# Attention in portions behind fixed VectorE and TensorE work, and other sums moved in a transformer block: a prediction and its test

## The chip, the cores and the metric

The kernel runs on one core of a Trainium2 chip. The metric is the device time of one execution in microseconds (us). The core has engines that work side by side, each through its own queue in order: TensorE (PE in the profile) multiplies matrices, VectorE (DVE) and ScalarE (ACT) work on elements, GpSimd (POOL) here mostly issues transfers (DMAs), SyncE (SP) here issues only transfers.

A ratio is the mean time of one kernel's fast runs over that of the kernel before in the same rounds on the same chip, so it is not quite the ratio of the medians that I quote beside it.

## The reference, cut to what matters

```python
xn = layernorm(x)                                   # 2048 tokens x 1024
q, k, v = split(xn @ wqkv)                          # 32 heads of 32
logits = einsum(q, k at 8 earlier positions, 2 apart) * 32**-0.5
attn   = softmax(logits)                            # over the 8 positions
s = einsum(attn, v at the same positions) @ wo
g = silu((silu(xn @ w1) * (xn @ w3)) @ w2)          # 1024 -> 3584 -> 1024
return x + s * g
```

The large products run on TensorE. Attention looks at only eight positions, so it has no large product: it is VectorE work.

## The kernel before

Tokens are handled in two halves of 1024, each half in two chunks of 512. The stages follow in this order: qkv, first up (w1 and w3), first down (w2), first wo; then the second half: up, wo, down. Every large product is done by Winograd's form of Strassen's scheme: seven products of half size in place of eight, with sums of the operands. VectorE makes these sums, also those of the weights, so VectorE stands between TensorE and its operands in each block:

```python
def seven(key, A, B, e11, e12, e22, e21, snap=None):      # one block: 56 matmuls
    ...
    for i in I: mm(pb[:, i], s2[i], t2, False)
    act_copy(su2[:], pb[:])
    for i in I: mm(pe[:, i], s4[i], b22, False)
    e12(pe, su2)          # VectorE: um = em + um;  in qkv: a pk sum
    for i in I: mm(pb[:, i], s3[i], t3, False)
    e22(pb, sp5)          # VectorE: h_sb = bm + pm;  in qkv: a pk sum
    def tail(): ...       # last product, into pb, three products later
```

`pe` and `pb` are PSUM tiles (PSUM is the memory that the matmuls write into). In the profile the first letter is that of the tile and the second that of the stage: `bm` and `em` are `pb` and `pe` of an up stage, `aq`, `bq` and `eq` tiles of qkv, and names with d or w in front tiles of down and wo. The tail writes into `pb`, so TensorE waits until the VectorE sum `h_sb` has read it; likewise `pe` comes free by `um`.

The queue order of an engine is made by a scheduler at build time. `issue_after` (here `behind`) holds an instruction behind another one in that order:

```python
def w_sums(fb):                      # sums of w1/w3 of block fb
    with behind(("m", fb - 1)):      # behind the um sum of the block before
        nc.vector.tensor_add(sa[:, 0], a21, a22)   # L547 in the profile
        ...                          # three more, then stores to s_dram

def w2_step(fb):                     # sums of w2, for two blocks at a time
    if fb % 2 == 0:
        ...                          # load two ring slots of w2
        return
    with behind(("t", fb)):          # behind the h_sb sum of block fb
        nc.vector.tensor_sub(o1, b12, b11)         # L618
        ...                          # three more, then the store to t_dram

def park(t, c, j0, name):            # q, k, v of chunks 1 to 3 go to HBM
    tl = k4(name, (2, CH), BF16)     # one of four small buffers
    def fin():
        m = nc.scalar.dma_start(out=dst, in_=tl[:])            # ACT's queue
        ...

def fetch_k(c):                      # k and q of a chunk come back
    nc.gpsimd.tensor_copy(out=kT[:, :, 0:HALO], in_=kT[:, :, CH:CH + HALO])
    nc.gpsimd.dma_start(out=kT[:, :, HALO:], in_=k_dram[c])
    qt[c] = att_tile((NJ, CH), BF16, f"qt{c}")
    nc.gpsimd.dma_start(out=qt[c][:], in_=q_dram[c])
```

The four small buffers that q, k and v pass through are called `pk` in the profile. A `pk` sum or copy writes one, so it has to wait until the store that last read this buffer has landed.

Attention is issued in a few large steps at a low priority (`priority(BG + ...)`), and VectorE takes them between the other sums as the scheduler decides. The weights go through a ring of nine slots: a slot is loaded again when its last reader, or the store of what was made in it, is done.

Of the kernel before, what the change touches and what calls it, by code (L numbers as in the profile page):

```python
# [17 lines left out]
def kernel(  # L18
# [126 lines left out]
    def mm(ps, lhs, rhs, first):  # L145
        n = len(lhs)
        for k in range(n):
            nc.tensor.matmul(  # L148
                ps, lhsT=lhs[k], rhs=rhs[k], start=(first and k == 0),
                stop=(k == n - 1), skip_group_check=not first,  # L150
            )
# [28 lines left out]
    def seven(key, A, B, e11, e12, e22, e21, snap=None):  # L180
# [27 lines left out]
        e22(pb, sp5)  # L208

# [119 lines left out]
    def park(t, c, j0, name):  # L329
        tl = k4(name, (2, CH), BF16)  # L330
        dst = (q_dram, k_dram, v_dram)[t][c, :, j0:j0 + 2, :]

        def fin():
            m = nc.scalar.dma_start(out=dst, in_=tl[:])
            if spill:
                d, f = spill.pop(0)
                with tc.issue_after(m.ins):
                    nc.scalar.dma_start(out=d, in_=f)

        return tl[:], fin  # L340
# [6 lines left out]
    def qkv_copy(t, c, j0):  # L347
        def f(ps, *a):
            d, fin = qkv_dst(t, c, j0)
            with hp():  # L350
                if a:
                    nc.vector.tensor_add(d, ps[:], a[0][:])
                else:
                    anchor["c", t, c, j0] = nc.scalar.copy(out=d, in_=ps[:])  # L354
                fin()
        return f
# [29 lines left out]

    def fetch_k(c):
        if c == 0:
            return
        nc.gpsimd.tensor_copy(out=kT[:, :, 0:HALO], in_=kT[:, :, CH:CH + HALO])  # L390
        nc.gpsimd.dma_start(out=kT[:, :, HALO:], in_=k_dram[c])
# [3 lines left out]
    def fetch_v(c):  # L395
        nc.gpsimd.tensor_copy(out=vT[:, :, 0:HALO], in_=vT[:, :, CH:CH + HALO])
        nc.gpsimd.dma_start(out=vT[:, :, HALO:], in_=v_dram[c])

    def scores(c):
        q = qt[c]  # L400
        E = att_tile((W, CH), BF16, f"Es{c}")
        for w in range(W):
            o = HALO - DIL * w
            p_t = att_tile((NJ, CH), BF16, f"pt{c}_{w}")
            nc.vector.tensor_mul(p_t[:], q[:], kT[:, :, o:o + CH])  # L405
            nc.vector.tensor_add(p_t[:, 0:4, :], p_t[:, 0:4, :], p_t[:, 4:8, :])  # L406
            nc.vector.tensor_add(p_t[:, 0:2, :], p_t[:, 0:2, :], p_t[:, 2:4, :])
            nc.vector.tensor_add(E[:, w, :], p_t[:, 0, :], p_t[:, 1, :])
        sc[c] = E

    def score_sums(c):
        E = sc[c]
        zp = bank2(f"zp{c}")
        for h in range(2):
            for sq in range(4):
                nc.tensor.matmul(
                    zp[sq * 32:(sq + 1) * 32, h].rearrange("p (w t) -> p w t", t=P), lhsT=ones4[:],
                    rhs=E[:, h * 4:(h + 1) * 4, sq * P:(sq + 1) * P], start=True, stop=True,
                )
        sc[c] = E[:].bitcast(FP32).rearrange("p w n -> p (w n)").rearrange("p (a w t) -> p a w t", a=2, t=P)  # L420
        nc.scalar.copy(out=sc[c][:, 0], in_=zp[:].rearrange("p h (w t) -> p (h w) t", t=P))

    def softmax(c):
        Z = sc[c]
        z, zm, zs = Z[:, 0], Z[:, 1, 0:4], Z[:, 1, 4:8]
# [4 lines left out]
        nc.scalar.activation(out=z, in_=z, func=ACTF.Exp, scale=scale)  # L430
# [8 lines left out]
    def values(c, pairs=(0, 2, 4, 6)):  # L439
        E = pr[c]  # L440

        def pvmul(dst, w):
            o = HALO - DIL * w
            nc.vector.tensor_mul(dst, E[:, w, :].unsqueeze(1).to_broadcast([P, NJ, CH]), vT[:, :, o:o + CH])  # L444

        A = oT[:, c % 2]
        for w0 in pairs:
            B = att_tile((NJ, CH), BF16, f"B{c}_{w0}")
            if w0 == 0:
                pvmul(A, 0)  # L450
                pvmul(B[:], 1)
            else:
                C = att_tile((NJ, CH), BF16, f"C{c}_{w0}")
                pvmul(B[:], w0)
                pvmul(C[:], w0 + 1)
                nc.vector.tensor_add(B[:], B[:], C[:])
            nc.vector.tensor_add(A, A, B[:])  # L457

    def att_steps():
        with priority(BG - 10000):  # L460
            scores(0)
        yield
        score_sums(0)
        fetch_k(1)
        with priority(BG):
            softmax(0)
            scores(1)
            values(0)
            fetch_v(1)
        yield  # L470
        with priority(BG + 9000):
            fetch_k(2)
        yield
        score_sums(1)
        with priority(BG + 10000):
            softmax(1)
            scores(2)
            values(1)
            fetch_k(3)
            fetch_v(2)  # L480
        yield
        score_sums(2)
        with priority(BG + 20000):
            softmax(2)
        yield
        with priority(BG + 30000), behind("wo"):
            scores(3)
            values(2, (0, 2, 4))
        yield
        score_sums(3)  # L490
        with priority(BG + 40000):
            softmax(3)
            values(2, (6,))
            fetch_v(3)
            values(3)
        yield

    att_it = att_steps()

    def att_step():  # L500
        next(att_it)
# [17 lines left out]
    def up_load(b, fb):  # L519
# [7 lines left out]
        else:  # L527
            up_sums(b, fb, w1t, w3t)
            sa, s4 = tiles[b, fb][2:]
            nc.sync.dma_start(out=sa[:], in_=s_dram[fb, :, 0:2])  # L530
            nc.sync.dma_start(out=s4[:], in_=s_dram[fb, :, 3])
# [3 lines left out]
    def up_sums(b, fb, w1t, w3t):  # L535
        sa = r4(("sa", fb), (2, KH, 2 * P), FP16)
        half.append(half.pop(0))
        s4 = slot(5, (KH, 2 * P), FP16, half[0] * SLOT // 2)
        tiles[b, fb] = w1t, w3t, sa, s4

    def w_sums(fb):
        up_sums(0, fb, *tiles[0, fb])
# [3 lines left out]
        with behind(("m", fb - 1)):  # L546
            nc.vector.tensor_add(sa[:, 0], a21, a22)  # L547
            nc.vector.tensor_sub(sa[:, 1], sa[:, 0], a11)
            nc.vector.tensor_sub(s4[:], a12, sa[:, 1])
            nc.vector.tensor_sub(s3, a11, a21)  # L550
# [11 lines left out]
    def mlp_up(b, steps={}):  # L562
        order = [*range(b * FB // 2, FB - 1), *range(b * FB // 2), FB - 1]
        for n, fb in enumerate(order):
            steps.get(n, lambda: None)()
            if n == 0:
                up_load(b, fb)
                if b == 0:
                    w_sums(fb)
                up_load(b, order[1])  # L570
# [8 lines left out]
            def e12(pe, su2):  # L579
# [5 lines left out]
                if b == 0:  # L585
                    anchor["m", fb] = m
                    if fb + 1 < FB:
                        w_sums(fb + 1)
                if n + 2 < FB:
                    up_load(b, order[n + 2])  # L590

            def e22(pb, sp5):
                with hp():
                    m = nc.vector.tensor_add(h_sb[:, f2, CH:], pb[:], sp5[:])  # L594
                if b == 0:
                    anchor["t", fb] = m
                    w2_step(fb)

            def e21(pb, f2=f2, hl=hl, n=n, fb=fb):
                release(("w3", fb))  # L600
                with hp():
                    nc.scalar.copy(out=hl["g"][:, :, 0:CH], in_=pb[:])  # L602
                    nc.vector.tensor_mul(h_sb[:, f2, :], h_sb[:, f2, :], hl["g"][:])  # L603

            seven(f"m{b}_{fb}", up_A(b, fb), B0, e11, e12, e22, e21)

    def w2_step(fb):
        if fb % 2 == 0:
            tiles["t"] = [r4("t", (2, 2, CH)) for x in range(2)]
            for x in range(2):  # L610
                nc.sync.dma_start(out=tiles["t"][x][:], in_=w2_q[:, fb:fb + 2, x])
            return
        q = tiles["t"]
        q16 = [t[:].bitcast(FP16) for t in q]
        b11, b12, b21, b22 = [q[x][:, :, y] for x in range(2) for y in range(2)]
        o1, o3, o4, o2 = [q16[x][:, :, y] for x in range(2) for y in range(2)]
        with behind(("t", fb)):
            nc.vector.tensor_sub(o1, b12, b11)  # L618
            nc.vector.tensor_sub(o3, b22, b12)
            nc.vector.tensor_sub(o2, b22, o1)  # L620
            nc.vector.tensor_sub(o4, b21, o2)
        for x in range(2):
            nc.gpsimd.dma_start(out=t_dram[:, fb - 1:fb + 1, 2 * x:2 * x + 2], in_=q16[x])
        release("t")
# [13 lines left out]
    def mlp_down(b, done=lambda *a: None, mid=lambda n: None):  # L638
        NQ = (0, 4, 8, 11, 14)

        def rhs_tiles(kind, fh=0, dh=0, t=0):
            key = kind, fh, dh, t
            ops = [key]
            for f0, f1 in zip(NQ, NQ[1:]):
                wt = r4(key, (f1 - f0, CH), FP16 if kind == "t" else BF16)
                if kind == "t":
                    nc.sync.dma_start(out=wt[:], in_=t_dram[:, f0:f1, t, :])
# [23 lines left out]
        def sums(gp):  # L671
# [3 lines left out]
            with hp():  # L675
                for g in G2:
                    nc.vector.tensor_add(s1[g], a21[g], a22[g])
                for g in G2:
                    nc.vector.tensor_sub(s3[g], a11[g], a21[g])

# [5 lines left out]
        for gp in G2:  # L686
            act_copy(pb[gp][:], pa[gp][:])
            with hp():
                nc.vector.tensor_sub(s2[gp], s1[gp], a11[gp])
        rhs = rhs_tiles("w", 1, 0)  # L690
        product(pa, lst(a12), rhs, False)
        rhs = rhs_tiles("t", t=T2)
        for gp in G2:
            with hp():
                nc.vector.tensor_sub(s4[gp], a12[gp], s2[gp])
# [5 lines left out]

        product(pb, lst(s2), rhs, False, snap2)
        mid(0)
        for gp in G2:
            with hp():
                silu(g_tile(b, 0, 0, gp), pa[gp][:])
            done(0, 0, gp)
        rhs = rhs_tiles("t", t=T3)
        product(pb, lst(s3), rhs, False)
# [3 lines left out]
        def c22(gp):  # L713
            sp5 = k4(f"dsp{b}_{gp}")
            act_copy(sp5[:], pe[gp][:])
            with hp():
                nc.vector.tensor_add(sp5[:], pb[gp][:], sp5[:])
                silu(g_tile(b, 1, 1, gp), sp5[:])
            done(1, 1, gp)

        product(pe, lst(s1), rhs, True, c22)
# [255 lines left out]
```

## Time and profile before

| | before |
|---|---|
| time, median of 3 runs | 754.03 us |
| span of the profiled run | 754.6 us |
| TensorE busy | 726.5 us, 96% |
| VectorE busy | 619.8 us, 82% |
| mean granted TensorE clock | 0.991 |

The profiled run took 756.28 us.

The head of the page of the kernel before: span, busy time of each engine with its share and number of instructions, and then the span in 40 slices, busy tenths for PE and DVE and the granted clock of TensorE in tenths.

```profile
span 754.6 us, 8791 instructions
...
PE 726.5 (96%) x3367; PEld 346.4 (46%) x3367; DVE 619.8 (82%) x602; ACT 312.9 (41%) x327; POOL 95.1 (13%) x156
...
PE   8999999889999999999899999999999999999997
...
DVE  7997996789999999999899558999984999552143
...
PEclk9999999999999999999999999999999999999999
```

TensorE is the bound, and it can only be won back where it stands still. The waits of PE of the kernel before: who waited for whom, total us, number of waits, the longest.

```profile
PE bm L148 <- DVE h_sb L594: 7.0, 9, 1.6
PE aq L148 <- ACT bq L158: 6.2, 3, 3.3
PE am L148 <- ACT bm L158: 2.3, 6, 0.5
PE da L148 <- DMA wring<-in_B_w_dram: 2.3, 1, 2.3
```

The first line is TensorE waiting for `h_sb`; VectorE had attention in front of it. The second is the end of qkv. The chain of waits of the kernel before in that stretch (start, duration, what) shows who was behind it:

```profile
135.20 4.94 DMA wring<-in_B_w_dram
...
140.23 0.06 DVE wring L547
...
143.04 1.23 DVE pk L352
...
144.35 1.01 ACT bq L158
...
145.40 1.89 PE aq L148 x8
```

VectorE's queue had the first weight sum (L547) ahead of a `pk` sum. The load of its weights took 4.9 us; then came the weight sum and an attention product of 2.3 us (L405, at 140.84 us), the `pk` sum stood behind both, and ACT and TensorE behind that. An instruction that waits at the head of an in-order queue holds up everything behind it. The Trainium skill says the same of these engines ("TensorE: Matmul & The Clock Gate", Part 1, on queue depths: VectorE is strict FIFO), and this chain agrees.

The stretches with a lower clock are three records of 3.4 us at clock 0.5, at 161, 366 and 529 us; such a stretch costs 1.7 us of TensorE work. They are called half clock below.

### The profile page before, as it was taken

The numbers are of one execution on the slowest core, as the hardware profiler recorded it, in microseconds if no ns is written. First come the engines' busy times: TensorE is split into PE (matmuls) and PEld (weight loads), VectorE is DVE, ScalarE is ACT, GpSimd is POOL, SyncE is SP. The second block draws the span as 40 slices with busy tenths as digits, with TensorE's granted clock in tenths as the row PEclk, the third lists the DMA queues.
The fourth block names the chain that finished last, engine by engine and source line by source line (L and its number), as shares of the span: only waits on it lengthen the run. The fifth ranks groups of instructions, "written<-read, shape, count | busy, mean of one in ns | idle before, by whom it ended". The sixth has DMA issues, their size and how long they took to land.

```text
span 754.6 us, 8791 instructions
## 1 busy us (share of the span) xinstructions
PE 726.5 (96%) x3367; PEld 346.4 (46%) x3367; DVE 619.8 (82%) x602; ACT 312.9 (41%) x327; POOL 95.1 (13%) x156
## 2 busy tenths in 40 slices
PE   8999999889999999999899999999999999999997
PEld 4655555444444444434344444444444444444443
DVE  7997996789999999999899558999984999552143
ACT  5744344435444555443021443443565454420121
POOL 0000001320211253411001402000022000000000
PEclk9999999999999999999999999999999999999999
DMA  8366358844778899979575978554367543624631
GB/s 324 122 153 197 125 168 294 271 146 166 230 244 258 274 320 303 308 243 330 190 229 182 354 228 282 163 162 129 121 183 235 152 132 120 209 83 140 207 115 56
DMA packets 130218, 153.68 MB, mean 204 GB/s; under 512 B 14976, under 2 KB 100480, under 8 KB 129536
## 3 DMA queue, kind: packets, MB, share of 16 engines
q1 hardware_dynamic: 112960, 102.25, 44.0%
q0 software_dynamic: 11024, 37.76, 14.8%
q10 hardware_dynamic: 6192, 13.11, 4.7%
q8 instruction: 26, 0.43, 0.2%
q14 instruction: 16, 0.13, 0.1%
HBM read 107.48 MB, written 39.32 MB: 195 GB/s over the span
## 4 chain that ended last, share of the span: by engine, by line
DVE 44%; PE 36%; issue 12%; DMA 5%; ACT 1%; POOL 0%; SPq 0%; DVEq 0%; ACTq 0%; POOLq 0%
PE bq L148 5%; DVE pt L405 5%; PE db L148 5%; PE da L148 5%; PE bm L148 4%; DVE B L444 3%; PE de L148 3%; DVE oT L457 3%; DVE um L581 3%; PE am L148 3%; DVE h_sb L594 3%; PE aq L148 3%; DVE pt L406 3%; PE eq L148 3%; PE em L148 3%
## 5 line engine op out<-in xcount | busy, mean ns | idle before, releaser
L148 PEld LDWEIGHTS <-wring 128*128 128x128 f16 (+1 forms) x1952 | 205.1, 105 | 232.1 <-issue 19.8
L148 PE MATMUL bm<-xs,wring 128*128 128x512 f16 x672 | 156.5, 380 | 7.1 <-DVE h_sb L594 7.0
L148 PEld LDWEIGHTS <-h_sb 128*128 128x128 f16 (+1 forms) x976 | 103.0, 106 | 121.7 <-issue 12.7
L148 PE MATMUL am<-xT,wring 128*128 128x512 bf16 x448 | 107.3, 382 | 2.3 <-ACT bm L158 2.3
L405 DVE TENSOR_TENSOR pt<-qt,kT 128x4096 bf16<-128x4096 bf16 x32 | 73.1, 2287 | 1.0 <-ACT kT L354 0.4
L148 PE MATMUL db<-wring,h_sb 128*128 128x512 f16 x336 | 73.3, 379 | 0.0
L583 ACT ACTIVATE g<-um 128x1024 bf16<-128x1024 f32 x28 | 29.6, 1057 | 86.4 <-DVE um L581 82.1
L437 POOL DMA_DIRECT2D Ep<-pb x64 | 37.0, 586 | 128.2 <-DVE pb L433 120.7
L148 PE MATMUL em<-xs,wring 128*128 128x512 f16 x224 | 52.9, 379 | 0.0
L148 PE MATMUL da<-wring,h_sb 128*128 128x512 bf16 x224 | 50.7, 388 | 2.3 <-DMA wring<-in_B_w_dram 2.3
L148 PE MATMUL em<-xT,wring 128*128 128x512 bf16 x224 | 52.9, 379 | 0.0
L603 DVE TENSOR_TENSOR h_sb<-h_sb,g 128x2048 bf16<-128x2048 bf16 x28 | 34.1, 1217 | 8.0 <-ACT g L602 8.0
L406 DVE TENSOR_TENSOR pt<-pt 128x2048 bf16<-128x2048 bf16 x32 | 38.9, 1219 | 0.4
L577 ACT ACTIVATE h_sb<-am 128x1024 bf16<-128x1024 f32 x28 | 28.7, 1024 | 21.5 <-PE am L148 21.5
L158 ACT COPY pm<-em 128x1024 f32<-128x1024 f32 x28 | 28.3, 1011 | 21.1 <-PE em L148 21.1
L581 DVE TENSOR_TENSOR um<-em,um 128x1024 f32<-128x1024 f32 x28 | 34.0, 1216 | 3.2 <-PE em L148 3.2
L158 ACT COPY um<-bm 128x1024 f32<-128x1024 f32 x28 | 28.4, 1014 | 19.9 <-PE bm L148 19.9
L457 DVE TENSOR_TENSOR oT<-oT,B 128x4096 bf16<-128x4096 bf16 x16 | 36.5, 2283 | 0.1
L444 DVE TENSOR_TENSOR B<-Ep,vT 128x4096 bf16<-128x4096 bf16 x16 | 36.4, 2282 | 0.0
L602 ACT CAST g<-bm 128x1024 bf16<-128x1024 f32 x28 | 28.3, 1012 | 16.1 <-PE bm L148 15.8
L594 DVE TENSOR_TENSOR h_sb<-bm,pm 128x1024 bf16<-128x1024 f32 x28 | 34.0, 1214 | 0.4 <-PE bm L148 0.4
L158 ACT COPY bm<-am 128x1024 f32<-128x1024 f32 x28 | 28.0, 1002 | 10.1 <-PE am L148 10.0
(180 smaller groups left out, 886.5 us busy)
## 6 DMA issues: line engine op xcount, KB each, us to landing
wring<-in_B_w_dram SPq DMA_DIRECT2D x68, 512.0 KB, 5.6
wring<-t_dram SPq DMA_DIRECT2D x16, 512.0 KB, 4.6
s_dram<-wring POOLq DMA_DIRECT2D x14, 512.0 KB, 3.7
s_dram<-wring POOLq DMA_DIRECT2D x28, 256.0 KB, 4.8
t_dram<-wring POOLq DMA_DIRECT2D x14, 512.0 KB, 6.9
wring<-s_dram SPq DMA_DIRECT2D x28, 256.0 KB, 3.1
wring<-s_dram SPq DMA_DIRECT2D x14, 512.0 KB, 3.9
wring<-in_A_wqkv_dram SPq DMA_DIRECT2D x6, 1024.0 KB, 7.5
```

Of the source, the lines that this page charges most:

```text
L148: nc.tensor.matmul(ps, lhsT=lhs[k], rhs=rhs[k], start=(first and k == 0), stop=(k == n - 1), skip_group_check=not first,)
L158: nc.scalar.copy(out=out_, in_=in_)
L405: nc.vector.tensor_mul(p_t[:], q[:], kT[:, :, o:o + CH])
L406: nc.vector.tensor_add(p_t[:, 0:4, :], p_t[:, 0:4, :], p_t[:, 4:8, :])
L437: nc.gpsimd.dma_start(out=pr[c][r:P:NR, :, sq * P:(sq + 1) * P], in_=pb[sq * 32:(sq + 1) * 32, :, :])
L444: nc.vector.tensor_mul(dst, E[:, w, :].unsqueeze(1).to_broadcast([P, NJ, CH]), vT[:, :, o:o + CH])
L457: nc.vector.tensor_add(A, A, B[:])
L577: nc.scalar.activation(out=h_sb[:, f2, 0:CH], in_=pa[:], func=ACTF.Silu)
L581: m = nc.vector.tensor_add(su2[:], pe[:], su2[:])
L583: nc.scalar.activation(out=hl["g"][:, :, CH:], in_=su2[:], func=ACTF.Silu)
L594: m = nc.vector.tensor_add(h_sb[:, f2, CH:], pb[:], sp5[:])
L603: nc.vector.tensor_mul(h_sb[:, f2, :], h_sb[:, f2, :], hl["g"][:])
```

## The change

Its intent: attention no longer comes in large steps, but in portions of so many us of VectorE work for each block of TensorE work, queued behind the block's fixed sums. The weight sums stand behind each block's first sum; the w2 sums are issued two blocks later; the stores of q, k, v go to SP's queue; the residual is copied into the output first and the results are added to it by the transfer; wo of the second half comes last. The core of the diff, with cuts marked by "...":

```diff
@@ seven
         e22(pb, sp5)
+        bg(pace["n"])
@@ park
-            m = nc.scalar.dma_start(out=dst, in_=tl[:])
+            m = nc.sync.dma_start(out=dst, in_=tl[:])
@@ attention
+    def bg(us):                       # issue about so many us of attention
+        ...
+        with priority(BG), behind("v"):
+            while pace["credit"] > 0:
+                t = next(att_it)
+                ...
-    def values(c, pairs=(0, 2, 4, 6)):
+    def values(c):                    # chunks 0 and 2 in two halves
+        ...
     def fetch_k(c):
-        nc.gpsimd.dma_start(out=kT[:, :, HALO:], in_=k_dram[c])
+        anchor["pool"] = nc.gpsimd.dma_start(out=kT[:, :, HALO:], in_=k_dram[c])
         qt[c] = att_tile((NJ, CH), BF16, f"qt{c}")
         nc.gpsimd.dma_start(out=qt[c][:], in_=q_dram[c])
@@ w_sums
-        with behind(("m", fb - 1)):
+        with behind("v"):
             nc.vector.tensor_add(sa[:, 0], a21, a22)
-            nc.vector.tensor_sub(sa[:, 1], sa[:, 0], a11)
-            ...
+        nc.vector.tensor_sub(sa[:, 1], sa[:, 0], a11)
+        ...
@@ mlp_up: in the tail of block fb
+                if b == 0:
+                    w2_sums(fb - 2)
+                    w2_load(fb)
@@ w2
-        with behind(("t", fb)):
-            nc.vector.tensor_sub(o1, b12, b11)
-            ...
+    def w2_sums(fb):                  # one block, half the width
+        ...
+        nc.vector.tensor_sub(o1, b12, b11)
+        ...
@@ results
-            nc.vector.tensor_add(g, g, xw[u, dh][:, gp])
-            nc.gpsimd.dma_start(out=out_rows(out_flat, 0, u, dh, gp), in_=g)
+            nc.gpsimd.dma_start(out=out_rows(out_flat, b, u, dh, gp), in_=g, accum_op=ALU.add)
@@ end of qkv k
-    xn_sums(xT1[:, 0], xT1[:, 1], xT1[:, 2], xT1[:, 3], xs1)
+    with behind("u"):
+        xn_sums(xT1[:, 0], xT1[:, 1], xT1[:, 2], xT1[:, 3], xs1)
@@ program
-    mlp_up(1, {0: att_step, 6: att_step})
-    wo_prepare(1)
-    wo(1, finish1)
-    residual()
-    mlp_down(1, gated)
+    pace["n"] = 8.3
+    mlp_up(1)
+    mlp_down(1, lambda: mid(1), (7, 10, 10, 9, 9, 3))
+    wo(1)
```

Note two things: the anchor of the w2 sums (`behind(("t", fb))`; an anchor is the instruction that another one is held behind) is taken away and has no successor, and nothing holds the load of q, whose line is unchanged.

## The prediction

> **What bounds the kernel now.** TensorE. The page's busy table has PE 96% busy (726.5 of 754.6 us), DVE 82%. In the chain of waits a product of 112 matmuls takes 24.17 us, 215.8 ns each, and both programs hold the same 3367 matmuls. So the change can only win time in which PE stands still or runs slowly. From the waits of PE and the timeline:
> - PE behind an ACT copy that waits for a late VectorE `pk` sum, at 142 and 157 us: 5.5 us. In the chain, VectorE's queue holds the MLP's first weight sum ahead of those `pk` sums, and that sum waits 4.9 us for weights.
> - PE behind the VectorE sum `h_sb` (bm<-h_sb), in both up stages: 7.0 us; behind ACT bm copies 2.3 us. VectorE is busy 20 of 20 us there (windows), with attention in front of the short sums.
> - PE in the first down product behind a weight load: 2.3 us; its ring slot waited for the w2 sums' store.
> - Three stretches of 3.4 us at half clock, at 161, 366 and 529 us, each just after such stalls (windows: granted clock 0.91): 1.7 us each. The Trainium skill, "TensorE: Matmul & The Clock Gate", Part 1, says the clock drops to half after an idle window of about 3.4 us; this trace shows drops after stalls of 2 us, and it decides.
> - Smaller ones, 2 us. Head (30 us) and tail (5.4 us after the last matmul) stay.
> Within reach: some 24 us. Floor near 730 us.
>
> **What the change does.** It issues attention in portions behind fixed sums, so that `pk`, `um`, `h_sb` are never behind more than about one 2.3 us operation. In the changed program's queue order the last `pk` sums stand before the first weight sum, and block 0's weights load earlier, between the q and v stores. w2 sums come two blocks late, so ring slots are free before down. wo of the second half goes last: same PE work.
> VectorE, with before's durations: residual sums fall away (-11 us); w2 sums at half width, 4 x 0.42 for one block instead of 4 x 0.68 for two, +4 us; values of chunks 0 and 2 in halves (1.22 instead of half of 2.28), +5 us. Net near zero.
> Balance of a block (PE: 56 x 0.2158 = 12.1 us): first up stage 3 x 1.22 + 4 x 0.68 + 4 x 0.42 + 4.5 attention = 12.5 us: slightly too much, I keep 2 to 3 us of stalls there. Second up stage 3.65 + 8.3 = 11.95: fits. Down: room for 7 to 10 us per product.
> Stores move from ACT's queue to SP's: ACT is no longer held up; weight loads can queue behind a store, estimated at no PE time.
> Tail: the last sum reads PSUM directly, in two halves; about the same 5.4 us. The earlier accumulating stores end, I estimate, shortly before it.
>
> **Result.** 754 - 7 (qkv end, with clock) - 4 (down) - 5 (second up stage, with clock) - 3 (first up stage, rest) = 735 us. Range 730 to 742. Chances: faster by over 2% 0.70, within 2% 0.28, slower 0.02.
>
> **What would show it.** PE waits at 140 to 160 us gone; da<-DMA gone; bm<-h_sb under 3 us; at most one half-clock stretch; DVE busy about 617 us, spread through the last 110 us; wo last, about 5 us before the end.
>
> **What would make it wrong.** A portion that waits (k, v or weights from DMA) at the head of VectorE's queue; SP holding weight loads behind a store; VectorE falling behind in the first up stage, each stall over 2 us costing another 1.7 us of clock; attention of chunk 1 or 3 late before wo; accumulating stores that end last.

## The result

| | before | changed |
|---|---|---|
| time, median (lowest to highest) | 754.10 us (753.07 to 754.72, 4 runs) | 759.37 us (757.82 to 760.22, 4 runs) |
| ratio, 95% interval | | 1.0069 (1.0048 to 1.009) |
| span of the profiled run | 754.6 us | 756.1 us |
| after the last matmul | 5.4 us | 7.8 us |

The changed kernel is 0.7% slower; I had put 735 us with a range up to 742. Executions over 1.5% slower than the fastest of the same kernel are left out of the means. The profiled run of the changed kernel is its fastest of four, and the profiled run of the kernel before is slower than its four, so the spans of the two profiles lie closer than the medians.

The head of the page of the changed kernel, the lines as before:

```profile
span 756.1 us, 8856 instructions
...
PE 724.1 (96%) x3367; PEld 346.7 (46%) x3367; DVE 619.6 (82%) x646; ACT 314.0 (42%) x326; POOL 110.1 (15%) x173
...
PE   8997999999998998998899999999999999999995
...
DVE  8984789589988888979799874696999799999515
...
PEclk9998999999999999999999999999999999999999
```

Busy times say nothing here: they are the same. The PE row says where to look: the right half is all nines, the left half has holes. The windows of the changed kernel (columns: PE, PEld, DVE, ACT and POOL busy us with instructions, granted clock, DMA share, GB/s) put numbers to it:

```profile
60.00:80.00 20.00, 15.59 (x62) 8.03 (x61) 11.53 (x10) 5.58 (x6) 0.00 (x0) 0.83 0.53 169
...
280.00:300.00 20.00, 16.59 (x70) 7.07 (x69) 16.92 (x23) 9.41 (x10) 2.70 (x5) 0.91 0.73 236
340.00:360.00 20.00, 16.83 (x71) 7.25 (x72) 18.50 (x21) 7.09 (x7) 6.22 (x11) 0.91 0.91 284
...
380.00:740.00 360.00, 359.94 (x1678) 162.57 (x1677) 293.06 (x235) 138.53 (x136) 42.37 (x54) 1.00 0.59 178
```

From 380 us on TensorE does not stand still for even 0.1 us in 360. The portions do there what they are meant to. What was won there and at the end of qkv was lost before 380 us, mostly to waits that the kernel before did not have. The waits of PE of the changed kernel:

```profile
PE em L148 <- DVE wring L604: 7.3, 3, 4.7
PE eq L148 <- DVE h_sb L289: 4.4, 1, 4.4
PE bm L148 <- DVE h_sb L650: 4.2, 2, 3.4
PE da L148 <- DMA wring<-in_B_w_dram: 2.6, 1, 2.6
...
PE bq L148 <- DVE pk L354: 1.4, 1, 1.4
```

and the two lines of the waits of DVE that stand behind them:

```profile
DVE wring L677 <- DMA wring<-in_B_w_dram: 17.1, 7, 4.7
...
DVE pk L354 <- DMA k_dram<-pk: 11.1, 1, 11.1
```

L677 is the first of the four w2 sums. VectorE stood 17 us at its head, waiting for w2 to be loaded. The timeline of DVE of the changed kernel shows one of these seven waits (start, duration, what, and in brackets the idle time before it):

```profile
231.28 1.22 DVE L638 TENSOR_TENSOR um<-em,um 128x1024 f32<-128x1024 f32 x1
232.41 0.68 DVE L604 TENSOR_TENSOR wring<-wring 128x1024 f16<-128x1024 bf16 x1
235.96 0.42 DVE L677 TENSOR_TENSOR wring<-wring 128x512 f16<-128x512 bf16 x1 [2.87 <-DMA wring<-in_B_w_dram]
236.30 1.22 DVE L650 TENSOR_TENSOR h_sb<-bm,pm 128x1024 bf16<-128x1024 f32 x1
```

This is the fifth L638 and the fifth L677: the w2 sum of the block stands between the block's own `um` and `h_sb`, not two blocks later. And `h_sb` (L650), for which TensorE waits, stands behind it. So does the weight sum L604 behind which TensorE waits longest: the w2 sum at 334.06 us came after a wait of 4.7 us, L604 only at 342.43 us, after work that had queued up meanwhile, and TensorE stood still from 338.5 to 343.2 us. The chain of waits of the changed kernel in the same stretch goes one step further back:

```profile
223.91 3.44 DMA s_dram<-wring
...
227.48 8.39 DMA wring<-in_B_w_dram
...
235.96 0.10 DVE wring L677
...
236.30 1.22 DVE h_sb L650
```

The w2 load waits for its ring slot, which comes free by the store of the block's weight sums. So w2 arrives late, in seven of the 14 blocks, and in this chain the wait starts in VectorE's own sums.

The second loss, at 69 us. The chain of waits of the changed kernel there:

```profile
54.29 1.24 DVE pk L354
55.52 2.63 SPq L286
...
59.42 7.44 DMA k_dram<-pk
...
67.75 1.23 DVE h_sb L289
...
69.02 1.04 PE eq L148 x2
```

L286 is a transfer on SP's queue that transposes the normalised x (a transposing load below); the k store now stands behind four of these. A later `pk` sum waits 11 us for the buffer that this store reads, and the xn sums (L289), which TensorE waits for, stand behind the `pk` sum. A stretch of 6.8 us at half clock begins at 67 us, within the stall.

The records of the granted clock of the changed kernel show half clock at 67 us (6.8 us) and at 289 and 344 us (3.4 us each): 13.6 us in all before the tail, against 10.2 us before.

### The profile page after: what moved, and what is told of

The parts are those of the page before. It is cut to its first block, busy times and chain, and to the rows that moved or that the text cites. A ratio compares the mean times of both kernels' runs of the same rounds, so it can differ in the third digit from the quotient of the medians.

```text
span 756.1 us, 8856 instructions
## 1 busy us (share of the span) xinstructions
PE 724.1 (96%) x3367; PEld 346.7 (46%) x3367; DVE 619.6 (82%) x646; ACT 314.0 (42%) x326; POOL 110.1 (15%) x173
## 4 chain that ended last, share of the span: by engine, by line
PE 74%; DVE 9%; DMA 8%; issue 5%; ACT 1%; POOL 1%; SPq 1%; DVEq 0%; POOLq 0%; ACTq 0%
PE bm L148 14%; PE em L148 10%; PE db L148 10%; PE am L148 9%; PE bq L148 6%; PE de L148 6%; PE da L148 6%; DMA wring<-in_B_w_dram 4%; PE eq L148 4%; PE aq L148 3%; PE wb L148 2%; DMA s_dram<-wring 2%; PE wa L148 2%; PE we L148 1%; DVE stats L244 1%
## 5 line engine op out<-in xcount | busy, mean ns | idle before, releaser
L469 DVE TENSOR_TENSOR BC<-Ep,vT 128x2048 bf16<-128x2048 bf16 (+1 forms) x42 | 65.1, 1573 | 0.2
L148 PE MATMUL em<-xs,wring 128*128 128x512 f16 x224 | 55.7, 394 | 7.3 <-DVE wring L604 7.3
L638 DVE TENSOR_TENSOR um<-em,um 128x1024 f32<-128x1024 f32 x28 | 34.1, 1219 | 15.1 <-PE em L148 13.0
L454 POOL DMA_DIRECT2D Ep<-pb x64 | 37.0, 588 | 56.9 <-PE bm L148 51.2
L479 DVE TENSOR_TENSOR oT<-oT,BC 128x2048 bf16<-128x2048 bf16 (+1 forms) x24 | 37.8, 1573 | 0.3
L650 DVE TENSOR_TENSOR h_sb<-bm,pm 128x1024 bf16<-128x1024 f32 x28 | 34.1, 1219 | 2.6 <-PE bm L148 2.6
L354 DVE TENSOR_TENSOR pk<-eq,uq 128x1024 bf16<-128x1024 f32 x12 | 14.7, 1222 | 25.6 <-PE eq L148 12.2
```

The costliest lines, as they stand in the source:

```text
L148: anchor["pe"] = nc.tensor.matmul(ps, lhsT=lhs[k], rhs=rhs[k], start=(first and k == 0), stop=(k == n - 1), skip_group_check=not first,)
L454: nc.gpsimd.dma_start(out=pr[c][r:P:NR, :, sq * P:(sq + 1) * P], in_=pb[sq * 32:(sq + 1) * 32, :, :])
L469: nc.vector.tensor_mul(dst, E[:, w, :].unsqueeze(1).to_broadcast([P, n, CH]), vT[:, js, o:o + CH])
L479: nc.vector.tensor_add(A, A, B if w0 else C)
L638: m = nc.vector.tensor_add(su2[:], pe[:], su2[:])
L650: m = nc.vector.tensor_add(h_sb[:, f2, CH:], pb[:], sp5[:])
```

## The experiments

In the edits below, "A" is the changed kernel and "B" the kernel before. My theory was that there are two misplacements: stores on SP behind the transposing loads, and w2 sums ahead of `h_sb`. The rivals: VectorE has too much work in the first up stage (12.5 us for 12.1 us of TensorE by my own sum in the prediction), or transfers get in each other's way. All kernels gave a correct result, except the one that is wrong on purpose.

| run | edit | median us | ratio (95%) |
|---|---|---|---|
| changed | | 759.37 | 1.0069 (1.0048 to 1.009) |
| a_store_act | A, stores on ACT's queue | 758.27 | 1.0069 (1.0039 to 1.0099) |
| a_w2_late | A, w2 sums behind the next block's h_sb | 738.34 | 0.9817 (0.9799 to 0.9835) |
| a_store1_w2 | the same, and stores of chunk 1 on ACT | 735.29 | 0.9764 (0.9748 to 0.978) |
| b_store_sp | B, stores on SP's queue | 750.46 | 0.9964 (0.9941 to 0.9987) |
| a_nou | A, xn sums without anchor | 755.01 | 1.0026 (0.9994 to 1.0059) |
| a_nou_w2 | a_w2_late and a_nou | 737.44 | 0.979 (0.9763 to 0.9816) |
| a_nou_store1_w2 | a_store1_w2 and a_nou | 740.82 | 0.9844 (0.9818 to 0.9871) |
| b_w2_free | B, w2 sums without anchor | 762.54 | 1.0127 (1.0097 to 1.0156) |
| a_qt | A, q load behind k load | 755.65 | 1.0029 (0.9997 to 1.0061) |
| a_qt_w2 | a_w2_late and a_qt | 737.07 | 0.9796 (0.9772 to 0.9821) |
| a_qt_w2_plain | the same, last stores do not add (wrong result) | 734.41 | 0.976 (0.9735 to 0.9785) |
| a_qt_w2_res | a_qt_w2, residual copy later | 740.03 | 0.9834 (0.9802 to 0.9865) |
| a_qtmid_w2 | a_w2_late, q load near 116 us | 732.75 | 0.9739 (0.9723 to 0.9755) |
| a_qtmid_nou_w2 | the same and a_nou | 732.18 | 0.9733 (0.9713 to 0.9753) |

### The w2 sums: a_w2_late and b_w2_free

```diff
@@ A, after the h_sb sum
+                if b == 0:
+                    anchor["h", fb] = m
@@ w2_sums
-        nc.vector.tensor_sub(o1, b12, b11)
+        with behind(("h", min(fb + 1, FB - 2))):
+            nc.vector.tensor_sub(o1, b12, b11)
```

> The changed kernel with each block's w2 sums held behind the next block's h_sb sum in VectorE's queue (at the latest behind that of block 12). Theory: the 17 us that VectorE waits for w2 loads fall below 3 us, em behind the weight sum (7.3 us), bm behind h_sb (4.2 us) and two half-clock stretches (3.4 us) nearly go: time 759 minus 10 to 15, 744 to 749. Rival (VectorE is overfull in the first up stage: 12.5 us of work for 12.1 us of TensorE in each block): only a third of it goes, time 754 or more, because the work itself is unchanged.

Measured: 738.34 us, 19 us by the ratios (1.0069 to 0.9817 of 754), more than I had put down. VectorE's waits for w2 loads fell from 17.1 to 2.1 us. In the waits of PE of this kernel the line of `em` behind the weight sum is gone, and of the 4.2 us behind `h_sb` 0.4 are left; the stall at 69 us stays.

```profile
PE eq L148 <- DVE h_sb L289: 4.5, 1, 4.5
...
PE da L148 <- DMA wring<-in_B_w_dram: 1.2, 1, 1.2
PE bq L148 <- DVE pk L354: 1.1, 1, 1.1
...
PE bm L148 <- DVE h_sb L650: 0.4, 1, 0.4
```

The same VectorE work in another order: the rival of the overfull VectorE falls. Two half-clock stretches went with the stalls; only the one at 69 us is left. The mirror of it takes the anchor from the kernel before:

```diff
@@ B, w2_step
-        with behind(("t", fb)):
+        with nullcontext():
```

> The kernel before with the anchor of its w2 sums taken away, so that the scheduler may place them as early as in the changed kernel; nothing else. Theory (the place of w2 sums in VectorE's queue is what costs): VectorE then waits for w2 loads 8 us or more and TensorE behind um, h_sb or weight sums in the first up stage by 5 us or more beyond the 5 us of before: time 753 plus 4 to 12. Rival (the harm is special to the changed kernel, its rings and loads): within 2 us of 753.

Measured: 762.54 us, 9.7 us slower, in the range given. VectorE waits 10.7 us for w2 loads. The timeline of DVE of this kernel has the longest one, and the waits of PE what it cost:

```profile
289.32 0.69 DVE L618 TENSOR_TENSOR wring<-wring 128x1024 f16<-128x1024 bf16 x1 [8.18 <-DMA wring<-in_B_w_dram]
...
291.83 1.22 DVE L581 TENSOR_TENSOR um<-em,um 128x1024 f32<-128x1024 f32 x1
292.97 0.68 DVE L547 TENSOR_TENSOR wring<-wring 128x1024 f16<-128x1024 bf16 x1
```

```profile
PE em L148 <- DVE wring L547: 10.0, 3, 7.8
```

The `um` sum and the weight sum L547 stand behind a w2 sum that waits 8.2 us, and TensorE waits 7.8 us for that weight sum. So the missing anchor does the same harm in a kernel that has nothing else of the change, though it costs about half as much there, 9.7 us in place of 19. That the place of the w2 sums is what costs is settled: one anchor, there and not there, in both kernels.

### The stores' queue: a_store_act, b_store_sp, a_store1_w2

```diff
@@ a_store_act: A, park          (b_store_sp is the reverse, in B)
-            m = nc.sync.dma_start(out=dst, in_=tl[:])
+            m = nc.scalar.dma_start(out=dst, in_=tl[:])
     ... and the same for the stores of x and xs
@@ a_store1_w2: A with the edit of a_w2_late, and
-            m = nc.sync.dma_start(out=dst, in_=tl[:])
+            m = (nc.scalar if t < 2 and c == 1 else nc.sync).dma_start(out=dst, in_=tl[:])
```

> The changed kernel with its q, k, v and spill stores back on ACT's queue, nothing else. Theory (two misplacements: stores queued on SP behind the four transposing loads, and w2 sums that stand in VectorE's queue ahead of sums whose turn it is): VectorE's 11.1 us wait for a k_dram store at 55 to 67 us falls below 2 us, the TensorE stall of 4.4 us at 69 us and its two half-clock windows go, time 759 minus 6 to 8, 751 to 753; the stalls of the first up stage stay. Rival (VectorE has too much attention in this stage, the queue of the stores is innocent): the stall at 69 us stays above 3 us and the time within 2 us of 759.

Measured: 758.27 us, no gain that the intervals show. The stall at 66 us shrank from 4.4 to 1.9 us, between what theory and rival had put down, but VectorE still waited 7.6 us for the k store, and another stall, of 2.1 us with half clock, came at the end of qkv.

> The kernel before with its stores on SP's queue, nothing else of the change. Theory (the queue of the stores alone makes the stall at 69 us): the same stall of 4 us or more appears near 69 us, with a half-clock window, time 754 plus 5 to 8. If stores on ACT's queue were what hurt the end of qkv, the stall of 5.5 us at 142 to 160 us falls at the same time; I expect it to stay, since VectorE's wait for weights makes it. Rival: no stall at 69 us, time within 2 us of 754 or lower.

Measured: 750.46 us, a little faster, and no stall above 0.7 us near 69 us. So my theory of the store's queue falls: it does no harm there alone. The second part of the expectation was wrong too: the stalls at 142 and 157 us did not stay, and one of 4.1 us with 6.8 us of half clock came at 165 us. In this kernel's timeline of DVE the `pk` sums (138.59 and 139.73 us) stand ahead of the weight sum (140.86 us), so the edit moved more than the stores: the order of VectorE's sums changed with it.

> Both mends: the q and k stores of chunk 1, those in the time of the transposing loads, go to ACT's queue, all other stores stay on SP's, and w2 sums behind the next block's h_sb. Theory: the gains add, 759 minus 17 to 22, 737 to 742, TensorE stalls after 30 us under 5 us in all. Rival (contention of transfers or too much VectorE work): less than 10 us gained.

Measured: 735.29 us, in the range, 0.5% better than a_w2_late. But a_store_act and b_store_sp forbid me to read that as the store's queue in general. Something else in the changed kernel had to make the store late.

### The anchor of the xn sums: a_nou, a_nou_w2, a_nou_store1_w2

```diff
@@ A
-    with behind("u"):
+    with nullcontext():
         xn_sums(xT1[:, 0], xT1[:, 1], xT1[:, 2], xT1[:, 3], xs1)
```

> The changed kernel without the one anchor that holds the sums of the second half's xn (h_sb by four sums) behind the k sums of chunk 1; stores stay on SP's queue, w2 sums as changed. In VectorE's order this moves just those four sums ahead of one pk sum. New theory (the stall at 69 us needs both: a pk sum that waits 11 us for a buffer whose store is late, and the xn sums placed behind it): the stall of 4.4 us and its two half-clock windows go, time 759 minus 6 to 8, 751 to 753, although the late store is still there and VectorE still waits for it 4 us or more. Rival (the late store alone): the stall stays above 3 us.

Measured: 755.01 us, short of the 751 to 753 put down; by the ratios 3.2 us less than the changed kernel, with intervals that overlap. The stall of 4.4 us turned into two of 2.0 and 1.2 us, without half clock: the xn sums now stand first, but they themselves wait 4.8 us for a transposing load.

> w2 sums held behind the next block's h_sb, and the xn sums' anchor taken away. Theory: the gains add to the 738.3 us of the first alone: minus 5 to 7, 731.5 to 733.5; TensorE stalls from 30 us on under 4 us in all, no half-clock window before the tail. Rival for the size: if a stall only moves to the next wait, time 735 or more.

Measured: 737.44 us: not the 731.5 to 733.5 put down. The rival for the size was right: the stall went to the next wait (2.3 us at 69 us, with its half clock).

> As the run before it, with the q and k stores of chunk 1 on ACT's queue too. Theory: with the xn sums ahead of it, the late store harms nothing, so within 1 us of that run. Rival (the store's queue counts by itself): 2 us or more faster.

Measured: 740.82 us, a miss on both sides: slower than a_nou_w2. The xn sums waited 9.5 us for the transposing loads, of which the last landed at 64.9 us, against 60.4 us in a_nou_w2. With stores on ACT's queue these loads were later in three kernels; why, I did not find out. But all three pointed to one thing: the last transposing loads are late in every descendant of the changed kernel so far. They landed at 60.5 us in the changed kernel, at 56.5 us in b_store_sp, which shares the stores' queue. (In the kernel before they landed at 60.3 us, as late. But there the k stores did not stand behind them: issued on ACT's queue, they had landed by 59.5 us.)

### The load of q: a_qt, a_qt_w2, a_qtmid_w2, a_qtmid_nou_w2

In the changed kernel POOL issues the 1 MB load of q for chunk 1 at 52 us; in the kernel before at 117 us. Nothing in the new source holds it, and q is in HBM by then. At 52 us the last two transposing loads run.

```diff
@@ a_qt: A, fetch_k
-        nc.gpsimd.dma_start(out=qt[c][:], in_=q_dram[c])
+        with behind("pool"):                  # behind the load of k
+            nc.gpsimd.dma_start(out=qt[c][:], in_=q_dram[c])
```

> The changed kernel with the load of q for chunk 1 (1 MB, issued at 52 us there, at 117 us before) held behind the load of k for the same chunk; nothing else. Third theory for the stall at 69 us: this load runs beside the last two transposing loads and makes them land after 7 us in place of 3.3, and the stores behind them on SP's queue go late with them. Expected: the last transposing load lands before 57 us in place of 60.5, TensorE's stall there below 1.5 us, no half-clock window before the first up stage, time 759 minus 5 to 8. Rivals (the store's queue; the anchor of the xn sums): the stall stays above 3 us, since both are still as changed.

Measured: 755.65 us. The last transposing load landed at 56.9 us, 3.1 us after its issue in place of 7.0, and the k stores behind it started at 55.8 us in place of 58.9. TensorE's stall there is 0.9 us and no half clock follows, although the store's queue and the anchor were as in the changed kernel. Only the start of the store moved: each k store takes 7.4 to 7.6 us in both kernels (7.7 in b_store_sp, 3.5 in the kernel before; why is not shown), and VectorE still waits 7.6 us for it, in place of 11.1. The time missed its range: by the ratios 3 us less than the changed kernel in place of 5 to 8, since stalls of 1.0 and 2.0 us came at 148 and 167 us, and the wait at 370 us (2.7 us, 2.6 in the changed kernel) was now followed by half clock.

Here is the timeline of SP in the changed kernel, and then in a_qtmid_w2 (below), where the q load is elsewhere too: the same four transposing loads hold SP 9.0 us in the one and 5.7 us in the other, and the k stores behind them start at 58.9 and 55.7 us.

```profile
49.17 8.98 SPq L286 DMA_TRANSPOSE h_sb<-wring  x4
...
58.87 0.93 SPq L335 DMA_DIRECT2D k_dram<-pk  x2
```

```profile
49.28 5.66 SPq L286 DMA_TRANSPOSE h_sb<-wring  x4
...
55.66 0.95 SPq L335 DMA_DIRECT2D k_dram<-pk  x2
```

The Trainium skill ("DMA: Bandwidth & Descriptors", "Issuing engines are not separate DMA queues") says that transfers issued by SP, ACT and POOL run on the same 16 DMA engines and interleave. This agrees: with the load from POOL's queue beside them the last two loads from SP's took 7.4 and 7.0 us (changed kernel), without it 3.2 and 3.1 (a_qt).

So the stall of 4.4 us takes both: the stores on SP's queue without the early q load left 0.7 us (b_store_sp) and 0.9 us (a_qt), the early q load with the stores on ACT's queue 1.9 us (a_store_act).

> The same, and w2 sums held behind the next block's h_sb. Theory: 738.3 minus 5 to 7 of the w2 run alone, 731 to 734, TensorE stalls after 30 us under 4 us in all, no half-clock window before the tail. If the stall at 69 us only turns into another wait: 736 or more.

Measured: 737.07 us, again the gain did not add. The stall near 69 us was down to 1.1 us, and others came up at 148 us (1.3 us) and 167 us (2.1 us, with half clock). Behind the k load the q load now ran from 134.9 to 145.1 us, beside the v stores and the first MLP weights; a v store, issued at 136.4 us, landed 8.9 us later, where the same store took 6.3 us in a_w2_late and, as it turned out, 6.4 us in a_qtmid_w2. The `pk` buffers came free late, and a `pk` sum waited 9.1 us for one. The same harm at another place, though with more traffic around it. So the next two kernels put the load where little else runs:

```diff
@@ a_qtmid_w2: A with the edit of a_w2_late, and
@@ park
             m = nc.sync.dma_start(out=dst, in_=tl[:])
+            anchor["st", t, c, j0] = m
@@ fetch_k
-        nc.gpsimd.dma_start(out=qt[c][:], in_=q_dram[c])
+        if c == 1:
+            with behind(("st", 2, 1, 2)):     # behind a v store
+                nc.sync.dma_start(out=qt[c][:], in_=q_dram[c])
+        else:
+            nc.gpsimd.dma_start(out=qt[c][:], in_=q_dram[c])
```

> w2 sums behind the next block's h_sb, and the load of q for chunk 1 on SP's queue between the v stores, near 105 us: away from the transposing loads (52 us), and away from the k load and the first MLP weights (135 us, where a_qt_w2 put it). Theory (a 1 MB load beside the stores that pk buffers wait for is what stalls TensorE, wherever it stands): TensorE stalls of 60 to 175 us fall below 3 us with no half-clock window before the tail; ratio to before 0.972 to 0.976, against 0.982 of w2 alone and 0.980 of a_qt_w2. Rival (the stall only moves on again): ratio 0.979 or more.

Measured: 732.75 us, ratio 0.9739, as the theory had it (the load was issued at 116 us, as in the kernel before). TensorE's stalls from 60 to 175 us are 1.0 us at 66 us and 1.0 us at 165 us, and there is no half-clock stretch between 6 and 726 us. It beats the kernel before by 2.6%. The edit changes two things about the load, its time and its queue (SP's in place of POOL's); no run parts them.

> The same without the anchor that puts the xn sums behind a pk sum. Theory: with the transposing loads early, the xn sums start at 57 us and the stall of about 1 us at 66 us goes too; ratio 0.970 to 0.975. Rival (the anchor costs nothing by then): within 0.002 of the run before it.

Measured: 732.18 us, ratio 0.9733. The stall at 66 us went, another of 0.2 us came at 68 us, and the one at the end of qkv grew to 1.6 us. Within 0.002: the anchor has no part of its own that these runs can show.

### The tail and the first down product: a_qt_w2_plain, a_qt_w2_res

```diff
@@ a_qt_w2_plain: the stores of the second half's first six results
-            nc.gpsimd.dma_start(..., in_=g, accum_op=ALU.add)
+            nc.gpsimd.dma_start(..., in_=g)
@@ a_qt_w2_res
-            if c == 0:
-                residual(0)
             yield from values(c + 1)
+            if c == 0:
+                residual(0)
```

In this expectation "the run before it" is a_qt_w2.

> Wrong result on purpose (second half without the residual): as the run before it, but the stores of the second half's first six results do not add to what lies in memory. Theory (the adding stores slow the last four stores): the last four land within 1.8 us of issue as before, in place of 2.3 to 3.4, and the time falls by 1 to 1.5 us against the run before it. Rival (the tail is VectorE's and the number of stores): change under 0.4 us.

Measured: 734.41 us, 2.7 us less than a_qt_w2 (ratios 0.976 and 0.9796, so 0.36%, with intervals that just overlap), more than the 1 to 1.5 us put down. In the profiles the time after the last matmul fell from 8.0 to 5.7 us. Of this profile's tail, the lines of the DMA view for the last four stores, a_qt_w2 first and then a_qt_w2_plain (size of each, median us from issue to landing):

```profile
out_dram<-h_sb SPq DMA_DIRECT2D x4, 128.0 KB, 4.0
```

```profile
out_dram<-h_sb SPq DMA_DIRECT2D x4, 128.0 KB, 1.9
```

In the kernel before these four took 1.7 us. The adding stores of the product before are what makes the last plain stores late.

> As a_qt_w2, with the copy of x into the output (first half, 2 MB) issued after the values of chunk 1 in place of before them. Theory (the copy runs beside the last weights of the first down product and makes them late): TensorE's wait for that load, 1.2 us, goes, and the time falls by 1 us. Rival (the load is late because its ring slot is): the wait stays within 0.3 us.

Measured: 740.03 us, 3 us slower in the medians, with ratio intervals that overlap. The wait for the weight load did not go (2.0 us with half clock, against 0.9 us in a_qt_w2), so that theory falls, and the copy now ran beside the wo weights, for which TensorE waited 2.8 us. In a_qtmid_w2 that wait for the weight load was gone without any edit aimed at it. What bounds it stays open.

Not tried: more than four `pk` buffers, which should take the waits for a `pk` buffer away without touching a transfer. A fifth does not fit: the build stops, since 20 KB of memory for each partition are asked for and 16.1 KB are left.

## Why the prediction was wrong, point by point

- **"w2 sums come two blocks late, so ring slots are free before down."** This step failed. In the source they are issued two blocks late; in VectorE's queue they stand in the block itself, ahead of its `h_sb` sum, since nothing anchors them. On the chip the load is late: it waits for a slot that a store frees. So VectorE waited 17.1 us for w2 loads, and TensorE behind it. Cost: 19 us, by the ratio of a_w2_late. I had the queue order before me, and read in it the order of `pk` and the weight sums only.
- **"`pk`, `um`, `h_sb` are never behind more than about one 2.3 us operation."** The same step, as a size. I counted what VectorE has to do ahead of these sums, not what it may have to wait for. The waits at the head of its queue were up to 4.7 us (w2) and 11.1 us (a `pk` buffer).
- **"Weight loads can queue behind a store, estimated at no PE time."** I watched the stores' effect on loads, not the loads' effect on stores. The harm ran the other way: stores started late behind loads that had gone slow, and `pk` sums waited for them. The queue alone made no stall at 69 us (b_store_sp); what set it off is the q load, issued 65 us sooner than before. I had seen it in neither list. Cost: 6 us, by the ratios of a_w2_late and a_qtmid_w2.
- **First up stage "slightly too much, I keep 2 to 3 us of stalls there".** Mis-sized. With the w2 sums in place the stage shows 0.4 us of waits behind `h_sb`, with the same VectorE work. VectorE was busy for 150.1 of 161.5 us there (a_w2_late, 178 to 339.5 us), 11.2 us for each 12.1 us of TensorE and not 12.5. I had added durations; in the timeline weight sums of 0.68 us start 0.60 us apart.
- **Tail "about the same 5.4 us".** 7.8 us; the adding stores slow the last ones, 2.3 us after the last matmul and 2.7 us in the medians by a_qt_w2_plain.
- **"da<-DMA gone", 4 us with its clock.** It stayed, 2.6 us, though without a half-clock stretch of its own. Not settled.
- **What held.** The end of qkv: 5.5 us of stalls and a half-clock stretch became 1.4 us, with no such stretch. The second up stage: no waits at all. TensorE as the bound, and equal TensorE and VectorE work. The half clock, in part: stalls of 4.4, 3.4 and 4.7 us in the changed kernel brought it on, those under 1.5 us never, but one of 2.6 us did not, so "each stall over 2 us" was too strong. I overlooked what parts them. The half-clock stretches of a profile begin whole multiples of 3.41 us apart. Cut the time into pieces of 3.41 us at these points and add up TensorE's stalls (those over 0.1 us) in each: in the 16 profiles 28 pieces at full clock, after the head and before the tail, held 2.0 us or more, and half clock followed each; the largest sum that it did not follow is 1.8 us. The 2.6 us stall lay across a cut (1.0 and 1.7 us), and so did the stall of 3.3 us at 142 us of the kernel before (1.7 and 1.6 us).
- **The clock term.** Three half-clock stretches, 5 us, were counted from one profiled run with a clock of 0.991. Over its span that clock loses 6.8 us, and the 0.996 that is the median of the 35 later runs 3.0 us. So my estimate is that 3 to 4 us of the predicted gain were not there to win in most of these runs.

Put together: a_qtmid_w2 is the change with its two oversights mended, and it takes 732.75 us; by its ratio that is 734.4 us on the base of 754.1, where I had predicted 735 for the change itself. That it comes so close is partly luck: the clock term was too large, the tail was 2 us worse, and the first up stage won more than I had put down. But the expected gain could be had; the change as made turned it into new waits in the first half.

## What to carry to other kernels

Where an engine works through its queue in order, ask of each instruction ahead of a critical one not only how long it takes but what it may wait for, down to the store that frees its load's buffer; "issued later" in the source is no place in the queue, so anchor it and check the order. An anchor that a change takes away, or a transfer that nothing holds, is a change of its own: look up where each transfer starts before and after. And when a stall is mended and the time stays, look where the same transfer went: here three mends of one stall each fed the next wait, until the load stood where little else ran.

## What the Trainium skill lacked or had wrong

- "TensorE: Matmul & The Clock Gate", Part 1: it says that the clock halves after an idle window of about 3.4 us, and that the window is free-running. The second agrees with the 3.41 us pieces above; the first is too strict. A window need not be idle throughout: 2.0 us of stalls in one were enough in each of 28 cases, and up to 1.8 us never were. So a single stall of 2.1 us (a_qt_w2 at 167 us) cost a further 1.7 us, and one of 3.3 us across two windows (the kernel before at 142 us) did not.
- "DMA: Bandwidth & Descriptors" says that issuing engines share the DMA engines, but gives no size for a transposing load beside a plain one. Here a 1 MB load took the last two transposing loads from 3.2 and 3.1 to 7.4 and 7.0 us, and held up SP's queue at issue: 9.0 us for four of them in place of 5.7.
- The same page says which engine must issue an accumulating transfer and warns of races, but I found no time for it there. Here adding stores made the plain stores after them land in 4.0 us in place of 1.9, and the time was 2.7 us longer in the medians.
